# A fused attention and gated convolution kernel: rope in nine GpSimd pieces, and three steps moved between engines

## The chip, the cores and the metric

The kernel runs on one core of a Trainium2 chip. A core has a matrix engine (TensorE, PE in the profile, whose weight loads stand apart as PEld), a vector engine (VectorE, DVE), a scalar engine for activation functions (ScalarE, ACT), a general engine (GpSimd, POOL) and a sync engine that issues transfers (SyncE, SP). Each works through its own queue in order; semaphores tie the queues together. The metric is device microseconds of one execution, as the median of several.

## The reference

Attention over 4 batches of 8 heads, 576 positions and 64 values per head, followed by a gated feed-forward layer:

```python
q_rot, k_rot = (rotate(q), rotate(k))          # rope: cos and sin of position
scores = scale * np.matmul(q_rot, k_rot.transpose(0, 1, 3, 2))
scores = scores - np.max(scores, axis=-1, keepdims=True)
attn = np.exp(scores)
attn = attn / (np.sum(attn, axis=-1, keepdims=True) + 1e-09)
x = np.matmul(attn, v)                          # heads side by side: 512 columns
h = np.maximum(x @ w_in, 0.0)                   # 512 -> 1024
conv_out = sum(conv_w[k] * hp[:, k:k + S, :])   # three taps along the sequence, hp is h padded
gate = 1.0 / (1.0 + np.exp(-conv_out))
return h * gate @ w_out                         # 1024 -> 512
```

Activations are 32-bit floats; the weights arrive as 64-bit floats and are turned on the chip.

## The kernel before

Heads are worked on in pairs, 16 pairs `p`, each in five steps `s` of 128 (the last 64) query rows. A step computes scores on PE (`emit_S`, line 232, into the PSUM tile `sp`), the negated row maximum on DVE (line 240), the exponential with its row sums on ACT (line 244, `st`), and turns the result on PE (`emit_T`, line 289) for ACT to copy out to `pt` (line 170, by `evac`). When a pair's steps are done, `emit_E` multiplies by the values (line 342, two halves, each ending with products that need the remainder rows `pt[:, 8]`, which DVE copies out of PSUM in `emit_Trem`, line 172), `emit_rinv` takes the reciprocal of the row sums on DVE (lines 315, 316), `emit_rinvT` turns it on PE and sends it through DRAM, and the norm on DVE (line 354) applies it.

Ahead of this, a pair's q and k are loaded by SP into `rq` and `rk`, rotated in place on GpSimd by `rope` (line 163 multiplies 1152 columns by the table, line 164 adds two halves into 576 columns), and turned by DVE into `qT` and `kT` (lines 209, 213). `qT` is then scaled in place on ACT (line 170, out and in both `qT`).

The feed-forward layer works in 8 blocks `blk` of 288 rows and 8 slices `f` of 128 hidden columns. `emit_M1` (line 373) makes a slice in three passes, ACT applies the relu into one of four `rr` tiles (line 381), DVE runs the three taps of the convolution (line 385 the first, line 387 the other two), ACT the tanh that makes the gate (line 393), DVE the product with h (line 396), and ACT and GpSimd split it into a high and a low part (lines 404, 405) for `emit_M2` (line 451).

The order is written out by hand: `at(n, rank, fn)` puts a piece of work into step `n` at a rank, and every emission on PE calls `tick`, which first emits what `defer(k, fn)` put off by `k` ticks. So a rank or a lag sets the place in each engine's queue, not a time. Steps below `WIDE` = 26 (about the first 150 us) hold attention and the conversion of the weights on ACT, DVE and GpSimd (lines 469 to 530); from there on attention and feed-forward slices alternate; the last blocks run alone at the end. `late["short"]` is set for the last steps and chooses shorter lags there.

Of the kernel before, what the change touches and what calls it, by code (L numbers as in the profile page):

```python
# [11 lines left out]
AF = mybir.ActivationFunctionType  # L12
ALU = mybir.AluOpType
# [7 lines left out]
def attention_moe_kernel(ctx, tc, q, k, v, w_in, conv_w, w_out, tab, tabx, out):  # L21
    nc = tc.nc
# [7 lines left out]
    HS = S // 2  # L30
# [4 lines left out]
    scale = float(D) ** -0.5  # L35
# [21 lines left out]
    tabt = keep.tile([128, S // 32, 2, 32], F32, name="tabt")  # L57
    idf = keep.tile([128, 128], F32, name="idf")
    cw = keep.tile([128, 32], F32, name="cw")
# [14 lines left out]
    late = {"tail": False, "short": False}  # L74
# [4 lines left out]
    def defer(k, fn, rank=1):  # L79
        due.setdefault(slot[0] + k, []).append((rank, len(due.get(slot[0] + k, [])), fn))  # L80
# [9 lines left out]
    def m_tile():  # L90
        if late["tail"]:
            return psum["t"].tile([128, 512], F32, tag="mt", name="mt")
        return psum["m"].tile([128, 512], F32, tag="m", name="pm")
# [66 lines left out]

    def rope(p, part):
        x = raw[p, part]
        nc.gpsimd.tensor_tensor(out=x, in0=x, in1=tabt, op=ALU.mult)  # L163
        nc.gpsimd.tensor_tensor(out=x[:, :, 0, :], in0=x[:, :, 0, :], in1=x[:, :, 1, :], op=ALU.add)

    QT, KT = {}, {}

    def evac(eng, out, in_, sc=None):
        if eng == "A" or "m" not in psum:
            nc.scalar.activation(out=out, in_=in_, func=AF.Copy, scale=1.0 if sc is None else sc)  # L170
        elif sc is None:
            nc.vector.tensor_copy(out, in_)
        else:
            nc.vector.tensor_scalar(out=out, in0=in_, scalar1=sc, scalar2=None, op0=ALU.mult)

    def qk_tiles(p):
        if p not in QT:
            QT[p] = p2.tile([128, S], F32, tag="qT", name="qT")
            KT[p] = p2.tile([128, S + 64], F32, tag="kT", name="kT")

    def k_rem(p):
        if p * STEPS < WIDE:
            for h in range(2):
                r = slice(64 * h, 64 * h + 64)
                evac("V", krem[p % 2][r, r], KT[p][r, 576:640])
# [19 lines left out]
    def emit_TQ(p, part):  # L205
        qk_tiles(p)
        x = raw.pop((p, part))[:, :, 0, :]
        if part == "q":
            nc.vector.transpose(out=QT[p].rearrange("p (c i) -> p c i", i=32), in_=x)
            defer(1, lambda: evac("A", QT[p], QT[p], scale))  # L210
        else:
            kt = KT[p].rearrange("p (c i) -> p c i", i=32)
            nc.vector.transpose(out=kt[:, 2:20], in_=x)
            nc.vector.transpose(out=kt[:, 0:2], in_=x[:, 16:18])
            k_rem(p)
# [5 lines left out]
    def go(d, key):  # L221
        for fn in d.pop(key):
            fn()
# [89 lines left out]
    def emit_rinv(p):  # L313
        s = p % 2
        nc.vector.tensor_scalar(out=sums[p], in0=sums[p], scalar1=1e-9, scalar2=None, op0=ALU.add)
        nc.vector.reciprocal(out=rvc[s][:, 0:9], in_=sums[p])
# [46 lines left out]
    def emit_M1(blk, f):  # L363
        b, j = divmod(blk, 2)
        g, rr = late["g"], late["rr"]
        ps = m_tile()
        fs = slice(128 * f, 128 * f + 128)
        n = 3 * NK
        i = 0
        for kk in range(NK):  # L370
            xs = xslot[b, kk, j]
            for w, e in ((winh, 0), (winh, 1), (winl, 0)):
                nc.tensor.matmul(  # L373
                    out=ps[:, 0:XW], lhsT=w[:, kk, fs], rhs=xT[:, xs, e, :], start=(i == 0), stop=(i == n - 1)
                )
                i += 1
        if f == NF - 1:
            for kk in range(NK):
                free_slots.append(xslot.pop((b, kk, j)))
        r = rr[(blk * NF + f) % len(rr)]  # L380
        nc.scalar.activation(out=r[:, 1:XW], in_=ps[:, j:j + XW - 1], func=AF.Relu)  # L381
        c = late["pc"].tile([128, HS], F32, tag="c", name="c")

        def conv():
            nc.vector.tensor_scalar(out=c, in0=r[:, j:j + HS], scalar1=cw[:, f:f + 1], scalar2=None, op0=ALU.mult)  # L385
            for e in (1, 2):
                nc.vector.scalar_tensor_tensor(  # L387
                    out=c, in0=r[:, j + e:j + e + HS], scalar=cw[:, 8 * e + f:8 * e + f + 1], in1=c,
                    op0=ALU.mult, op1=ALU.add,
                )  # L390

        def tanh():
            nc.scalar.activation(out=c, in_=c, func=AF.Tanh, scale=0.5)  # L393

        def gate():
            nc.vector.scalar_tensor_tensor(  # L396
                out=c, in0=c, scalar=1.0, in1=r[:, j + 1:j + 1 + HS], op0=ALU.add, op1=ALU.mult
            )

        def split():  # L400
            o = 0
            for dst, n in g_pieces(blk, f):
                hi, lo = dst[:, 0, :], dst[:, 1, :]
                nc.scalar.activation(out=hi, in_=c[:, o:o + n], func=AF.Copy)  # L404
                nc.gpsimd.tensor_tensor(out=lo, in0=c[:, o:o + n], in1=hi.bitcast(F32), op=ALU.subtract)  # L405
                o += n
            ready.add((blk, f))

        lag = (1, 2, 3, 4) if late["short"] else (2, 5, 7, 9)
        for k, fn in zip(lag, (conv, tanh, gate, split)):  # L410
            defer(k, fn)

# [157 lines left out]
    def at(n, rank, fn):  # L570
        plan.setdefault(n, []).append((rank, len(plan.get(n, [])), fn))

    def emit():
        with tc.manual_schedule(engines=engines):
# [17 lines left out]
            for p in range(1, NP):  # L592
                n = STEPS * p
# [6 lines left out]
            for p in range(NP):  # L600
                n = STEPS * p
                for s in range(STEPS):
                    m = n + s
                    first = m < WIDE
                    if m:
                        at(m - 1 if first else m, 0.5 if first else 0, lambda p=p, s=s: emit_S(p, s))
                    at(m, 0.2, lambda p=p, s=s: go(reds, (p, s)))
                    at(m, 0.3 if first else 1.5, lambda p=p, s=s: go(exps, (p, s)))
                    for h in range(2 if s < 4 else 1):
                        at(m + 1, 0 if m + 1 < WIDE else 1, lambda p=p, s=s, h=h: emit_T(p, s, h))  # L610
                for g, e in ((0, 2), (1, 4), (2, 5)):
                    at(n + e, 2, lambda p=p, g=g: emit_Trem(p, g))
                at(n + 4, 4, lambda p=p: emit_E(p, 0))
                at(n + 5, 4, lambda p=p: emit_E(p, 1))
                at(n + 5, 1.7, lambda p=p: emit_rinv(p))
                at(n + 6, 2, lambda p=p: emit_rinvT(p))
                for j in range(2):
                    at(n + 8, 1.7 + j, lambda p=p, j=j: norms.pop((p, j))())
            nw = len(wsteps)
            for i, u in enumerate(wsteps):  # L620
                x = (WIDE - 1) * i // nw
# [120 lines left out]
```

## Time and profile before

| What | Value |
|---|---|
| median of 3 runs | 581.32 us (576.83 to 585.36) |
| profiled execution | 585.31 us, of which the span of instructions is 583.2 us |
| granted TensorE clock, mean | 0.959 |
| PE busy | 513.9 us (88%) |
| DVE busy | 417.5 us (72%) |
| ACT busy | 316.6 us (54%) |
| POOL busy | 241.3 us (41%) |

Busy time is the sum of the spans in which an engine works on an instruction; whatever an instruction waits for after it has started counts as busy. The clock is a share of 2.4 GHz, and is 0.5 in some stretches. Within a stretch the views tell what each engine idled for, and the instruction that ended the idle time.

### The profile page before, as it was taken

How to read it: one execution, taken by the hardware profiler on the slowest of the kernel's cores; microseconds unless marked ns; L12 is line 12 of the kernel's file. 1: busy time of each engine (PE TensorE's matmuls, PEld its weight loads, DVE VectorE, ACT ScalarE, POOL GpSimd, SP SyncE). 2: the span in 40 equal slices, each digit the busy share in tenths (PEclk: the TensorE clock that was granted, in tenths of full speed). 3: DMA queues.
4: the chain of work that ended last, by engine and by line, in shares of the span. 5: the costliest groups of instructions: out<-in, count | busy, mean ns of one | idle time of the engine just before them, and what ended most of it. 6: DMA issues, size and time to landing. Idle time of an engine off the chain costs nothing.

```text
span 583.2 us, 9069 instructions
## 1 busy us (share of the span) xinstructions
PE 513.9 (88%) x3160; PEld 364.0 (62%) x3160; DVE 417.5 (72%) x668; ACT 316.6 (54%) x810; POOL 241.3 (41%) x221
## 2 busy tenths in 40 slices
PE   3597879788895999897998899997998999999997
PEld 1253434344664667674777577674866767779986
DVE  4888778784586958878598848877288847466971
ACT  2678676675654655565546545574255646334530
POOL 3636547554363534427071714545044212142440
PEclk9979989998896999999999989997999999999999
DMA  9774663934422315051513214060240101000001
GB/s 216 138 155 117 150 143 90 197 75 82 81 42 57 67 50 92 8 113 22 113 28 83 59 54 88 17 124 1 77 83 21 41 22 39 22 37 19 1 36 55
DMA packets 138385, 42.51 MB, mean 73 GB/s; under 512 B 131004, under 2 KB 131940, under 8 KB 138340
## 3 DMA queue, kind: packets, MB, share of 16 engines
q1 hardware_dynamic: 136996, 41.54, 32.6%
q8 instruction: 25, 0.41, 0.3%
q10 hardware_dynamic: 1344, 0.39, 0.3%
q14 instruction: 20, 0.16, 0.1%
HBM read 37.12 MB, written 4.79 MB: 72 GB/s over the span
## 4 chain that ended last, share of the span: by engine, by line
PE 58%; DVE 21%; ACT 9%; DMA 5%; issue 4%; SPq 3%; DVEq 0%; ACTq 0%
PE sp L232 12%; PE pm L451 9%; PE tp L342 8%; PE pm L373 8%; PE tp L289 8%; PE mt L451 6%; DVE c L387 5%; PE mt L373 4%; DVE negm L240 4%; DVE c L385 3%; ACT st L244 3%; DVE c L396 2%; ACT pt L170 2%; DMA w<-moe_w_in 1%; DMA rq<-q 1%
## 5 line engine op out<-in xcount | busy, mean ns | idle before, releaser
L170 ACT ACTIVATE pt<-tp 128x512 f32<-128x512 f32 (+2 forms) x164 | 86.3, 557 | 102.7 <-PE tp L289 98.4
L240 DVE TENSOR_REDUCE negm<-sp 128x1 f32<-128x576 f32 x144 | 102.7, 749 | 42.3 <-PE sp L232 41.8
L405 POOL TENSOR_TENSOR g<-c,g 128x288 fp32r<-128x288 f32 (+4 forms) x88 | 56.2, 650 | 169.9 <-ACT g L404 163.6
L232 PE MATMUL sp<-kT,qT 64*128 64x288 f32 (+4 forms) x556 | 111.3, 490 | 15.9 <-ACT st L244 15.9
L244 ACT ACTIVATE st<-sp,negm 128x576 f32<-128x576 f32 x128 | 93.4, 739 | 14.4 <-DVE negm L240 10.7
L387 DVE SCALAR_TENSOR_TENSOR c<-rr,cw,c 128x288 f32<-128x288 f32 x128 | 91.7, 717 | 4.5
L289 PE MATMUL tp<-idf,st 128*128 128x128 f32 x512 | 78.6, 294 | 17.8 <-ACT st L244 11.5
L289 PEld LDWEIGHTS tp<-idf,st 128*128 128x128 f32 x512 | 58.1, 147 | 47.2 <-ACT st L244 17.4
L373 PE MATMUL pm<-xT,winh 128*128 128x290 f32 x384 | 84.5, 312 | 0.5 <-ACT rr L381 0.5
L232 PEld LDWEIGHTS sp<-kT,qT 64*128 64x128 f32 (+1 forms) x556 | 49.5, 184 | 54.4 <-ACT st L244 25.0
L342 PE MATMUL tp<-pt,vm 128*64 128x290 f32 x512 | 71.7, 423 | 3.7 <-ACT pt L170 3.4
L359 POOL TENSOR_TENSOR xT<-xn,xT 128x290 fp32r<-128x290 f32 x32 | 27.5, 880 | 94.2 <-ACT xT L358 92.9
L373 PEld LDWEIGHTS pm<-xT,winh 128*128 128x128 f32 x384 | 62.8, 194 | 1.4 <-ACT rr L381 0.7
L451 PE MATMUL pm<-wouth,g 128*128 128x512 f32 x176 | 62.2, 411 | 0.0
L396 DVE SCALAR_TENSOR_TENSOR c<-c,rr 128x288 f32<-128x288 f32 x64 | 48.6, 759 | 16.8 <-ACT c L393 16.5
L385 DVE TENSOR_SCALAR c<-rr,cw 128x288 f32<-128x288 f32 x64 | 47.4, 741 | 14.8 <-ACT rr L381 14.5
L373 PE MATMUL pm<-xT,winl 128*128 128x290 f32 x192 | 57.5, 300 | 0.0
L342 PEld LDWEIGHTS tp<-pt,vm 128*64 128x64 f32 x512 | 34.7, 140 | 30.0 <-ACT pt L170 5.1
L163 POOL TENSOR_TENSOR rq<-rq,tabt 128x1152 f32<-128x1152 f32 x15 | 40.5, 2700 | 5.5 <-DMA rq<-q 5.5
L393 ACT ACTIVATE c<-c 128x288 f32<-128x288 f32 x64 | 28.4, 444 | 22.6 <-DVE c L387 22.3
L163 POOL TENSOR_TENSOR rk<-rk,tabt 128x1152 f32<-128x1152 f32 x15 | 40.5, 2701 | 0.0
L451 PEld LDWEIGHTS pm<-wouth,g 128*128 128x128 f32 x176 | 33.5, 190 | 9.7 <-issue 2.2
(99 smaller groups left out, 761.9 us busy)
## 6 DMA issues: line engine op xcount, KB each, us to landing
out<-ot SPq DMA_DIRECT2D x17, 256.0 KB, 2.1
rq<-q SPq DMA_DIRECT2D x30, 144.0 KB, 3.2
rq<-q SPq DMA_DIRECT2D x60, 72.0 KB, 2.9
rk<-k SPq DMA_DIRECT2D x30, 144.0 KB, 3.1
rk<-k SPq DMA_DIRECT2D x60, 72.0 KB, 2.9
w<-moe_w_in SPq DMA_DIRECT2D x8, 512.0 KB, 5.0
vm<-v SPq DMA_DIRECT2D x32, 128.0 KB, 2.5
w<-moe_w_out SPq DMA_DIRECT2D x8, 512.0 KB, 4.2
```

Source lines behind the costliest of these rows:

```text
L163: nc.gpsimd.tensor_tensor(out=x, in0=x, in1=tabt, op=ALU.mult)
L170: nc.scalar.activation(out=out, in_=in_, func=AF.Copy, scale=1.0 if sc is None else sc)
L232: nc.tensor.matmul(out=out, lhsT=qt[64 * h:64 * h + 64, c], rhs=kt[64 * h:64 * h + 64, a:a + n], start=True, stop=True)
L240: reds.setdefault((p, s), []).append(lambda: nc.vector.tensor_reduce(out=nm, in_=sc, axis=AX.XY if len(sc.shape) == 3 else AX.X, op=ALU.ma ...
L244: lambda: nc.scalar.activation(out=dst, in_=sc, func=AF.Exp, bias=nm, scale=1.0, accum_out=sm)
L289: nc.tensor.transpose(ps[:, 128 * t:128 * t + 128], st[:, 128 * t:128 * t + 128], idf)
L342: nc.tensor.matmul(out=xp[64 * h:64 * h + 64, 0:XW], lhsT=vmain[p][:, h, i, :] if i < 4 else vrem[:, h, :], rhs=PT[p][:, 2 * i + h if i < ...
L373: nc.tensor.matmul(out=ps[:, 0:XW], lhsT=w[:, kk, fs], rhs=xT[:, xs, e, :], start=(i == 0), stop=(i == n - 1))
L385: nc.vector.tensor_scalar(out=c, in0=r[:, j:j + HS], scalar1=cw[:, f:f + 1], scalar2=None, op0=ALU.mult)
L387: nc.vector.scalar_tensor_tensor(out=c, in0=r[:, j + e:j + e + HS], scalar=cw[:, 8 * e + f:8 * e + f + 1], in1=c, op0=ALU.mult, op1=ALU.add,)
L396: nc.vector.scalar_tensor_tensor(out=c, in0=c, scalar=1.0, in1=r[:, j + 1:j + 1 + HS], op0=ALU.add, op1=ALU.mult)
L451: nc.tensor.matmul(out=ops[tt][:, 0:width], lhsT=g_tile(tt, f, e), rhs=w[:, f, cols], start=(f == 0 and i == 0), stop=(f == NF - 1 and i = ...
```

## The change

Four edits. `rope` is issued as six multiplications of 192 columns and three additions of 6 x 32 columns in place of one of 1152 and one of 576. The scaling of `qT` is put off by five ticks in place of one. The first tap of the convolution is an ACT activation with a scale per partition one tick after the relu, in all but the last steps, and the lags of what follows go from (2, 5, 7, 9) to (2, 4, 5, 6). The reciprocal of the sums moves from rank 1.7 to rank 4.5 of its step.

```diff
--- before.py
+++ after.py
@@ -160,8 +160,12 @@
 
     def rope(p, part):
         x = raw[p, part]
-        nc.gpsimd.tensor_tensor(out=x, in0=x, in1=tabt, op=ALU.mult)
-        nc.gpsimd.tensor_tensor(out=x[:, :, 0, :], in0=x[:, :, 0, :], in1=x[:, :, 1, :], op=ALU.add)
+        for a in range(0, 18, 3):
+            y = x[:, a:a + 3]
+            nc.gpsimd.tensor_tensor(out=y, in0=y, in1=tabt[:, a:a + 3], op=ALU.mult)
+        for a in range(0, 18, 6):
+            y = x[:, a:a + 6]
+            nc.gpsimd.tensor_tensor(out=y[:, :, 0, :], in0=y[:, :, 0, :], in1=y[:, :, 1, :], op=ALU.add)
 
     QT, KT = {}, {}
 
@@ -207,7 +211,7 @@
         x = raw.pop((p, part))[:, :, 0, :]
         if part == "q":
             nc.vector.transpose(out=QT[p].rearrange("p (c i) -> p c i", i=32), in_=x)
-            defer(1, lambda: evac("A", QT[p], QT[p], scale))
+            defer(5, lambda: evac("A", QT[p], QT[p], scale))
         else:
             kt = KT[p].rearrange("p (c i) -> p c i", i=32)
             nc.vector.transpose(out=kt[:, 2:20], in_=x)
@@ -381,8 +385,14 @@
         nc.scalar.activation(out=r[:, 1:XW], in_=ps[:, j:j + XW - 1], func=AF.Relu)
         c = late["pc"].tile([128, HS], F32, tag="c", name="c")
 
+        def tap():
+            nc.scalar.activation(out=c, in_=r[:, j:j + HS], func=AF.Copy, scale=cw[:, f:f + 1])
+
+        short = late["short"]
+
         def conv():
-            nc.vector.tensor_scalar(out=c, in0=r[:, j:j + HS], scalar1=cw[:, f:f + 1], scalar2=None, op0=ALU.mult)
+            if short:
+                nc.vector.tensor_scalar(out=c, in0=r[:, j:j + HS], scalar1=cw[:, f:f + 1], scalar2=None, op0=ALU.mult)
             for e in (1, 2):
                 nc.vector.scalar_tensor_tensor(
                     out=c, in0=r[:, j + e:j + e + HS], scalar=cw[:, 8 * e + f:8 * e + f + 1], in1=c,
@@ -406,7 +416,9 @@
                 o += n
             ready.add((blk, f))
 
-        lag = (1, 2, 3, 4) if late["short"] else (2, 5, 7, 9)
+        if not short:
+            defer(1, tap)
+        lag = (1, 2, 3, 4) if short else (2, 4, 5, 6)
         for k, fn in zip(lag, (conv, tanh, gate, split)):
             defer(k, fn)
 
@@ -612,7 +624,7 @@
                     at(n + e, 2, lambda p=p, g=g: emit_Trem(p, g))
                 at(n + 4, 4, lambda p=p: emit_E(p, 0))
                 at(n + 5, 4, lambda p=p: emit_E(p, 1))
-                at(n + 5, 1.7, lambda p=p: emit_rinv(p))
+                at(n + 5, 4.5, lambda p=p: emit_rinv(p))
                 at(n + 6, 2, lambda p=p: emit_rinvT(p))
                 for j in range(2):
                     at(n + 8, 1.7 + j, lambda p=p, j=j: norms.pop((p, j))())
```

The order of DVE's queue at the end of a pair, before the change (the 64x64 copy is of the remainder rows that the second half of `emit_E` needs; `rr_1323` and `rr_1324` are two of the four relu tiles, `c` the convolution):

```order
L396 SCALAR_TENSOR_TENSOR c<-c,rr_1323 128x288
L385 TENSOR_SCALAR c<-rr_1324,cw 128x288
L387 SCALAR_TENSOR_TENSOR c<-rr_1324,cw,c 128x288 x2
L240 TENSOR_REDUCE negm<-sp 128x1 x2
L315 TENSOR_SCALAR sums<-sums 128x9
L316 RECIPROCAL rvc_82<-sums 128x9
L172 COPY pt<-tp 64x64 x2
L396 SCALAR_TENSOR_TENSOR c<-c,rr_1324 128x288
```

and the same place in the changed kernel (line numbers are 4 to 12 higher; `rr_1407` and `rr_1408` are the same two relu tiles):

```order
L406 SCALAR_TENSOR_TENSOR c<-c,rr_1407 128x288
L176 COPY pt<-tp 128x256
L397 SCALAR_TENSOR_TENSOR c<-rr_1408,cw,c 128x288 x2
L244 TENSOR_REDUCE negm<-sp 128x1 x2
L176 COPY pt<-tp 64x64 x2
L406 SCALAR_TENSOR_TENSOR c<-c,rr_1408 128x288
L319 TENSOR_SCALAR sums<-sums 128x9
L320 RECIPROCAL rvc_82<-sums 128x9
```

The first tap has left the queue, and the copies now come straight behind the two maxima, with sums and reciprocal behind them.

The order of ACT's queue where a pair's `qT` is scaled, before:

```order
L170 ACTIVATE pt<-tp 128x4x128 x2
L404 ACTIVATE g<-c 128x224
L404 ACTIVATE g<-c 128x64
L170 ACTIVATE qT<-qT 128x576
L244 ACTIVATE st,sums<-sp,negm 128x576 x2
L170 ACTIVATE pt<-tp 128x4x128 x2
L244 ACTIVATE st,sums<-sp,negm 128x576 x2
L381 ACTIVATE rr_1321<-pm 128x289
L170 ACTIVATE pt<-tp 128x4x128 x2
L393 ACTIVATE c<-c 128x288
```

and now:

```order
L174 ACTIVATE pt<-tp 128x4x128 x2
L248 ACTIVATE st,sums<-sp,negm 128x576 x2
L174 ACTIVATE qT<-qT 128x576
L174 ACTIVATE pt<-tp 128x4x128 x2
L248 ACTIVATE st,sums<-sp,negm 128x576 x2
L385 ACTIVATE rr_1405<-pm 128x289
L389 ACTIVATE c<-rr_1405,cw 128x288
L174 ACTIVATE pt<-tp 128x4x128
L403 ACTIVATE c<-c 128x288
L174 ACTIVATE pt<-tp 128x4x128
```

The scaling stands behind the two exponentials, and the tap (line 389) stands behind its relu. The tanh (line 403) stands ahead of a copy to `pt` that it stood behind.

## Rows read from the trace of the kernel before

**Rows 1.** Two stretches: length, busy us (count) per engine, PEclk, DMA share, GB/s.

```profile
20.00:150.00 130.00, 102.36 (x576) 53.35 (x574) 101.05 (x148) 93.40 (x230) 74.75 (x47) 0.92 0.56 122
150.00:500.00 350.00, 324.61 (x2089) 237.38 (x2088) 253.82 (x402) 190.03 (x488) 134.79 (x129) 0.96 0.27 58
```

**Rows 2.** What PE waited for, 150 to 500 us: total, times, longest.

```profile
PE sp L232 <- ACT st L244: 13.9, 11, 6.4
PE tp L342 <- DVE pt L172: 8.6, 4, 2.5
PE tp L342 <- ACT pt L170: 2.8, 6, 0.5
```

**Rows 3.** Timeline, a pair ends: start us, us, engine, line, tiles, xcount, [idle <-releaser].

```profile
264.27 1.51 DVE L396 SCALAR_TENSOR_TENSOR c<-c,rr 128x288 f32<-128x288 f32 x1 [1.20 <-ACT c L393]
...
264.95 1.24 PE L232 MATMUL sp<-kT,qT 64*128 64x288 f32 x8
...
265.70 1.50 DVE L385 TENSOR_SCALAR c<-rr,cw 128x288 f32<-128x288 f32 x1
...
267.25 1.50 DVE L387 SCALAR_TENSOR_TENSOR c<-rr,cw,c 128x288 f32<-128x288 f32 x2
...
268.67 1.41 DVE L240 TENSOR_REDUCE negm<-sp 128x1 f32<-128x576 f32 x2
268.88 2.61 POOL L163 TENSOR_TENSOR rk<-rk,tabt 128x1152 f32<-128x1152 f32 x1
...
270.00 1.53 DVE L315 TENSOR_SCALAR sums<-sums 128x9 f32<-128x9 f32 x1
...
271.69 0.40 DVE L172 COPY pt<-tp 64x64 f32<-64x64 f32 x2
...
272.14 0.71 PE L342 MATMUL tp<-pt,vr 128*64 128x290 f32 x4 [2.51 <-DVE pt L172]
```

**Rows 4.** Timeline, the step after a pair ends.

```profile
301.19 0.80 POOL L405 TENSOR_TENSOR g<-c,g 128x288 fp32r<-128x288 f32 x1 [2.62 <-ACT g L404]
...
301.95 2.64 POOL L163 TENSOR_TENSOR rk<-rk,tabt 128x1152 f32<-128x1152 f32 x1
...
302.50 2.40 DVE L396 SCALAR_TENSOR_TENSOR c<-c,rr 128x288 f32<-128x288 f32 x1
...
304.83 1.51 DVE L385 TENSOR_SCALAR c<-rr,cw 128x288 f32<-128x288 f32 x1
...
307.90 1.42 DVE L240 TENSOR_REDUCE negm<-sp 128x1 f32<-128x576 f32 x2
...
310.04 0.68 ACT L170 ACTIVATE qT<-qT 128x576 f32<-128x576 f32 x1 [1.69 <-DVE qT L209]
...
310.63 0.72 ACT L244 ACTIVATE st<-sp,negm 128x576 f32<-128x576 f32 x1
...
311.50 1.96 PE L232 MATMUL sp<-kT,qT 64*128 64x288 f32 x8 [1.60 <-ACT st L244]
```

**Rows 5.** Timeline, two DVE operations while POOL is idle.

```profile
316.69 0.45 DVE L396 SCALAR_TENSOR_TENSOR c<-c,rr 128x288 f32<-128x288 f32 x1
...
317.75 1.07 DVE L387 SCALAR_TENSOR_TENSOR c<-rr,cw,c 128x288 f32<-128x288 f32 x2
```

**Rows 6.** Timeline, the start of a rope, and DVE beside it.

```profile
173.18 0.82 DVE L396 SCALAR_TENSOR_TENSOR c<-c,rr 128x288 f32<-128x288 f32 x1 [1.34 <-ACT c L393]
173.65 2.87 POOL L163 TENSOR_TENSOR rk<-rk,tabt 128x1152 f32<-128x1152 f32 x1
...
173.93 2.76 DVE L385 TENSOR_SCALAR c<-rr,cw 128x288 f32<-128x288 f32 x1
```

**Rows 7.** Groups by line and shape, ACT: count, busy us, mean ns, idle before.

```profile
L393 ACT ACTIVATE c<-c 128x288 f32<-128x288 f32 x64 | 28.4, 444 | 22.6 <-DVE c L387 22.3
```

**Rows 8.** Timeline, DVE turns a q in the first 150 us.

```profile
46.20 0.78 DVE L209 STREAM_TRANSPOSE qT<-rq 128x576 f32<-128x576 f32 x1 [1.30 <-POOL rq L164]
```

**Rows 9.** Stretch with a lowered clock (columns of rows 1).

```profile
400.00:409.00 9.00, 7.86 (x30) 5.37 (x31) 4.59 (x9) 3.48 (x9) 2.84 (x4) 0.62 0.00 0
```

## The prediction

> **What bounds the kernel now.** The page's busy shares come first: PE is busy for 88% of the span, DVE for 72%, ACT for 54%, POOL for 41%. So PE carries the time, and what can be gained is PE's idle time and the time that it works at a lowered clock. The view by stretches says where the idle time lies [rows 1]: from 20 to 150 us PE is busy for 102.4 of 130 us (27.6 idle), from 150 to 500 for 324.6 of 350 (25.4 idle). The diff leaves the feed-forward slices of the end as they were (the old branch for short lags), so the time after 500 us is left alone here.
>
> The view of waits breaks the 25.4 us down almost without remainder [rows 2]: scores wait for an exponential (13.9 us, 11 times, one of them 6.4), the second product with the values waits for DVE's copy of the remainder rows (8.6 us, 4 times), the first product for ACT's copies (2.8 us, 6 times). None of these names GpSimd. The timeline does. Where a pair ends, DVE takes 1.51 us for the gate product, 1.50 for the first tap and 1.50 for two more taps [rows 3]; with POOL idle the gate product takes 0.45, the two taps 1.07 together [rows 5]. In another pair the gate product starts at 302.50, inside a rope multiplication that runs from 301.95 to 304.59, takes 2.40 and ends 0.31 after it; the tap behind it is held up again, for 1.51 in all [rows 4]. So a DVE operation that meets a rope instruction stands still until it has nearly ended (0.45 of work against 0.31 of overhang: it starts some 0.14 us before the recorded end). Operations that read PSUM aren't held: maxima behind it run at 0.7 each [rows 3, 4].
>
> What follows from it is seen in the same rows. In rows 3 the scores are there at 264.95 + 1.24 = 266.2, but DVE gets to their maxima only at 268.67; behind these stands the sums' operation, 1.53 us beside the next rope; then the copy, and PE goes on at 272.14 after 2.51 us of idle time. In rows 4 the maxima end at 309.3, but ACT's exponential starts at 310.63, since the scaling of q stands ahead of it and had waited 1.69 us for DVE to turn q; PE goes on at 311.50 after 1.60 us.
>
> **The change, part by part.**
>
> Rope pieces. A GpSimd instruction of 288 columns takes 0.80 us, one of 1152 takes 2.64 [rows 4]: 1.84 / 864 = 2.13 ns a column, so 192 columns are 0.80 - 0.20 = 0.60 us. Nine are 5.4; the two old ones are 2.64 and, by the same line, 1.41, so a rope grows by 1.35 us, 30 ropes by 40 us. POOL is busy for 135 of 350 us [rows 1], and in that stretch nothing of rows 2 waits for it. A DVE operation that meets a piece now waits at most 0.60 - 0.14 = 0.46 us, at the least nothing; I take the upper end, since the operations of rows 3 and 4 stand close behind each other and the next piece starts when one is through. A gate product then costs 0.9, two taps 2.0.
>
> The copy's gap (rows 3, done again). From 264.27: gate product 0.9, the other copy that now stands here 0.4, two taps 2.0, so the maxima start at 267.6 and not at 268.67, and end at 269.0; the copy comes directly behind them, as the sums have moved, and ends at 269.4. PE was through with what came before at 272.14 - 2.51 = 269.6. The gap is gone. Of the 8.6 us I leave 0.6: **-8.0**, between -4 and -8.6.
>
> The exponential's gap (rows 4). From 302.50: gate product 0.9, two taps 2.0 without the first, sums and reciprocal 0.8, so maxima at 306.2 and through at 307.6; the scaling no longer stands ahead of the exponential, which starts at 307.7 and not at 310.63; PE's scores follow it by 0.9 as they do now, at 308.6, before PE is free for them (311.50 - 1.60 = 309.9). The gap is gone. The one long wait stands behind a rope beside which the first tap took 2.76 us [rows 6]: without that tap, and with 0.46 in place of a whole instruction for the taps behind it, some 4.5 of 6.4 us come back. Of the other 7.5 us I leave 1.0. **-11.0**, between -5.5 and -13.
>
> The tap on ACT. Five blocks of eight slices take it, 40 in all. An activation of this shape with constant operands takes 0.444 us [rows 7]; the tap has a scale per partition. At 576 columns the exponential, which has a bias per partition, takes 0.72 and the scaling of q, which has none, 0.68 [rows 4], so I add 0.04: 0.48 us, 19 us on ACT, whose 350 us hold 190 of work [rows 1]. That is hidden in its sum, but copies to `pt` stand behind tap and tanh now, and PE's 2.8 us of waits for them may double: **+2.8**, between 0 and +7 (0.48 us at a third of 40, or so).
>
> The Trainium skill speaks against this edit a little more strongly than the row: "ScalarE: Activation LUTs", What ACT_TABLE_LOAD costs, has each per-partition operand add about 93 ns. The rows say 40 ns, though one of them reads PSUM and the other doesn't; by that figure of the Trainium skill the tap would be an estimated 0.54 us, and the sum at most 2 us higher, were every tap on PE's path.
>
> Before 150 us. There is no tap yet, and the queue to turn q is tight: DVE already waited 1.30 us for a rope once [rows 8]. Five ropes of q, 1.35 us longer each, cost at most 6.8. On the other side a blocked conversion gets shorter, as the gate product of rows 4 does (2.40 to 0.9, 1.5 us), at most once for each of four pairs on the path: 6. I set the two against each other: 0, between -6 and +6.8.
>
> The clock. Behind PE's gaps stand stretches at 1.2 GHz: from 400 to 409 us the granted clock is 0.62, so 9 x 0.38 / 0.5 = 6.8 us at the lower level, with PE busy for 7.9 of the 9 [rows 9]. From 150 to 500 us the mean is 0.96 [rows 1], 28 us at the lower level; half of that, less the idle time inside, is lost, some 8 us. Fewer gaps may mean fewer of these: between 0 and -8, I take **-4**.
>
> The sum: 585.3 (the profiled execution) - 8.0 - 11.0 + 2.8 + 0 - 4 = 565.1. That execution lies 4.0 above the median of 581.3 and at the top of three that spread by 8.5; I take these 4.0 to be clock as well, so that against the median the clock's term is already in: 581.3 - 16.2 = 565.1 again. The predicted time is **565 us**, the range of this case 553 to 574.
>
> **The rivals.**
>
> *The gaps come back elsewhere.* DVE's wait gets shorter, but PE waits next for ACT, and the longer rope holds up q in the first 150 us. Half of the 19 us return and the 6.8 are lost: 581.3 - 9.5 + 6.8 = 578.6. For it: rows 8, and ACT's longer queue. Against it: both reconstructed gaps close with 0.2 to 1.3 us to spare. Chance 0.25.
>
> *DVE doesn't get in between the pieces*, so that the change doesn't do what it says. Then an operation waits for the whole 5.4 us in place of 2.64, while the one behind it is free (some 1.1 saved): 1.7 us more at each of 20 ropes, 34; with three quarters of it on the path, as the 15 gaps of 8.6 and 13.9 us suggest, +25, less 9 for the edits that don't hang on rope: 597. Against it: the multiplication starts at 173.65 [rows 6] straight behind another GpSimd instruction, and the gate product beside it, 0.82 from 173.18, still ended at 174.0, while the multiplication took 2.87 and not 2.64; the DVE operation had come in between. "GPSIMD Engine Reference", Instruction dispatch, in the Trainium skill lets each of the engine's cores start the next instruction as soon as its own share is done, with which there need be no moment between two pieces. By that rule it is this case; the trace disagrees in rows 6. Chance 0.05.
>
> *The gate waits for ACT*, which is the slower end. Its place in DVE's queue is now three ticks behind the taps and one behind the tanh, where it was five and two; maxima and copies stand behind it, and ACT has the tap to do. Such a wait is already there once in rows 3, 1.20 us. At 30 of 40 slices on the path this is 36 us: 565 + 36 = 601. It decides against the change when the tanh ends on average over 0.5 us after DVE is ready for the gate (40 x 0.5 = 20 us, all that was gained). Against it: maxima (1.4 us) stand between taps and gate at most places, and the tanh is 0.44. Chance 0.08.
>
> **The numbers.** 0.62 for the forecast, 0.25, 0.05 and 0.08 for the rivals. Two per cent of the median is 11.6 us, about what a measurement of this kernel can tell from no change. Below 569.7 lies most of the forecast's case (0.55) and a little of the first rival (0.02): 0.57 faster. Above 592.9 lie the second and third rival, nearly whole: 0.12 slower. The rest, 0.31, is within 2%. The range of 552 to 582 takes in the forecast's case and the larger part of the first rival.
>
> **What the profile after would show.** Right: rope pieces of about 0.60 us; taps with a mean of 0.6 to 0.7 and gate products of about 0.6, none over 1.1; PE waits from 150 to 500 us of about 8 us in place of 25; exponentials that start directly behind their maxima. The tap on ACT near 0.48. Wrong: DVE operations of 2 us and more beside a run of pieces (second rival); DVE idle before the gate, released by ACT's tanh, in tens of us (third); DVE idle before it turns q, released by POOL, of over 5 us (first). My forecast is most easily wrong by the waits on ACT, of which no row of before shows the new order.

## The result: 32 us faster, twice what was forecast

The changed kernel takes 548.71 us (median of 4 runs, 546.33 to 549.59) against 580.86 for the kernel before, run beside it: a ratio of 0.944 (95% interval 0.936 to 0.952), 32 us. The prediction was 565, with a range from 552: the direction and the mechanism came as forecast, but the forecast gain was only half of the measured one, and the time lies just below the range.

The profiled execution took 547.9 us, with a span of 546.1 (583.2 before). The first lines of its profile page:

```profile
span 546.1 us, 9259 instructions
PE 503.4 (92%) x3160; PEld 357.5 (65%) x3160; DVE 350.7 (64%) x628; ACT 331.0 (61%) x850; POOL 279.5 (51%) x431
```

PE's 3160 matmuls are the same ones. They took 513.9 us before and take 503.4 now: 10.5 us less for the same work, which is the clock (mean granted clock 0.959 before, 0.977 now). PE's idle time fell from 583.2 - 513.9 = 69.3 to 546.1 - 503.4 = 42.7, by 26.6. So 37.1 us of span are 26.6 of idle time and 10.5 of clock. (The medians differ by less, 32 us: the profiled execution of before is 4.4 us longer than its median.)

The two stretches that answer to [rows 1]: length, busy us (count) for PE, PEld, DVE, ACT, POOL, then granted clock, DMA share, GB/s.

```profile
20.00:150.00 130.00, 107.42 (x606) 56.83 (x604) 93.59 (x151) 94.80 (x233) 94.24 (x135) 0.91 0.58 125
150.00:500.00 350.00, 343.22 (x2274) 256.85 (x2272) 218.16 (x407) 215.36 (x561) 164.05 (x262) 1.00 0.27 60
```

From 150 to 500 us PE now idles for 6.8 us, not 25.4, at a mean clock of 1.00, not 0.96; DVE is busy for 36 us less. From 20 to 150 us it idles for 22.6, not 27.6, although POOL has 20 us more to do there.

What PE waited for from 150 to 500 us, which answers to [rows 2] (total, times, longest):

```profile
PE tp L346 <- ACT pt L174: 2.8, 6, 0.5
PE sp L236 <- ACT st L248: 2.0, 9, 0.5
```

The waits for DVE's copy (8.6 us) are gone altogether, those for the exponential fell from 13.9 to 2.0, those for ACT's copies stayed at 2.8. The 1.9 us that remain of 6.8 are three waits of the feed-forward layer, of the same lengths as three that before came after 500 us.

The timeline where the pair of [rows 3] ends (start us, us, engine, line, operation, tiles, shapes, count, idle time before it and its releaser; in order of start):

```profile
247.33 1.07 DVE L397 SCALAR_TENSOR_TENSOR c<-rr,cw,c 128x288 f32<-128x288 f32 x2 [1.34 <-ACT c L389]
...
247.99 3.82 POOL L165 TENSOR_TENSOR rq<-rq,tabt 128x192 f32<-128x192 f32 x6
...
248.75 1.42 DVE L244 TENSOR_REDUCE negm<-sp 128x1 f32<-128x576 f32 x2 [0.34 <-PE sp L236]
...
249.99 2.17 PE L346 MATMUL tp<-pt,vm 128*64 128x290 f32 x16 [0.47 <-ACT pt L174]
...
250.09 0.45 DVE L176 COPY pt<-tp 64x64 f32<-64x64 f32 x2
...
250.56 0.80 DVE L406 SCALAR_TENSOR_TENSOR c<-c,rr 128x288 f32<-128x288 f32 x1
...
251.28 0.56 DVE L319 TENSOR_SCALAR sums<-sums 128x9 f32<-128x9 f32 x1
...
251.99 0.66 PE L346 MATMUL tp<-pt,vr 128*64 128x290 f32 x4
```

DVE waits for scores at 248.4 now (0.34 us), where before the scores waited for DVE. The copy is done at 250.54, and PE comes to its rows at 251.99, straight out of other work: 1.4 us to spare. The gate product in the middle of six rope pieces takes 0.80, the sums 0.56, not 1.53.

The place of [rows 4]:

```profile
280.73 0.63 DVE L406 SCALAR_TENSOR_TENSOR c<-c,rr 128x288 f32<-128x288 f32 x1
...
283.12 1.64 DVE L397 SCALAR_TENSOR_TENSOR c<-rr,cw,c 128x288 f32<-128x288 f32 x2 [0.84 <-ACT c L389]
...
285.57 1.42 DVE L244 TENSOR_REDUCE negm<-sp 128x1 f32<-128x576 f32 x2
...
287.47 0.74 ACT L248 ACTIVATE st<-sp,negm 128x576 f32<-128x576 f32 x1
...
289.63 0.76 PE L236 MATMUL sp<-kT,qT 64*128 64x288 f32 x4
289.95 0.70 ACT L174 ACTIVATE qT<-qT 128x576 f32<-128x576 f32 x1
```

The exponential stands ahead of the scaling of q, and PE's next scores come 1.4 us after its end with no wait. The same operations by line and shape (count, busy us, mean ns, idle time before), first the taps and the gate product in the kernel before, then the changed kernel:

```profile
L387 DVE SCALAR_TENSOR_TENSOR c<-rr,cw,c 128x288 f32<-128x288 f32 x128 | 91.7, 717 | 4.5
L396 DVE SCALAR_TENSOR_TENSOR c<-c,rr 128x288 f32<-128x288 f32 x64 | 48.6, 759 | 16.8 <-ACT c L393 16.5
```

```profile
L397 DVE SCALAR_TENSOR_TENSOR c<-rr,cw,c 128x288 f32<-128x288 f32 x128 | 85.0, 664 | 39.6 <-ACT c L389 36.5
L406 DVE SCALAR_TENSOR_TENSOR c<-c,rr 128x288 f32<-128x288 f32 x64 | 35.2, 550 | 9.4 <-ACT c L403 9.1
L319 DVE TENSOR_SCALAR sums<-sums 128x9 f32<-128x9 f32 x16 | 7.3, 458 | 0.0
L389 ACT ACTIVATE c<-rr,cw 128x288 f32<-128x288 f32 x40 | 21.6, 539 | 0.2
L165 POOL TENSOR_TENSOR rq<-rq,tabt 128x192 f32<-128x192 f32 x90 | 56.0, 655 | 6.1 <-DMA rq<-q 6.1
```

A tap costs 0.66 us on the mean (0.72 before) and a gate product 0.55 (0.76 before); beside an idle POOL they take 0.53 and 0.45 [rows 5]. A new wait stands in the first line: DVE idles for 36.5 us in all for ACT's tap. No wait of PE follows from it, and the kernel that keeps the tap on DVE is as fast (the first experiment below).

### The profile page after: what moved, and what is told of

Read it like the earlier page. It is cut to its first block, busy times and chain, and to the rows that moved or that the text cites. A ratio compares the mean times of both kernels' runs of the same rounds, so it can differ in the third digit from the quotient of the medians.

```text
span 546.1 us, 9259 instructions
## 1 busy us (share of the span) xinstructions
PE 503.4 (92%) x3160; PEld 357.5 (65%) x3160; DVE 350.7 (64%) x628; ACT 331.0 (61%) x850; POOL 279.5 (51%) x431
## 4 chain that ended last, share of the span: by engine, by line
PE 69%; ACT 9%; DVE 6%; DMA 4%; issue 4%; SPq 3%; POOL 3%; POOLq 0%; DVEq 0%; ACTq 0%
PE sp L236 14%; PE tp L346 13%; PE pm L463 11%; PE pm L377 10%; PE tp L293 9%; PE mt L463 6%; PE mt L377 5%; ACT pt L174 4%; ACT st L248 3%; POOL rq L165 2%; DVE negm L244 1%; DVE c L397 1%; SPq L125 1%; DMA rq<-q 1%; PE tp L305 1%
## 5 line engine op out<-in xcount | busy, mean ns | idle before, releaser
L236 PE MATMUL sp<-kT,qT 64*128 64x288 f32 (+4 forms) x556 | 108.5, 484 | 3.0 <-ACT st L248 3.0
L397 DVE SCALAR_TENSOR_TENSOR c<-rr,cw,c 128x288 f32<-128x288 f32 x128 | 85.0, 664 | 39.6 <-ACT c L389 36.5
L293 PE MATMUL tp<-idf,st 128*128 128x128 f32 x512 | 75.2, 285 | 14.6 <-ACT st L248 8.4
L293 PEld LDWEIGHTS tp<-idf,st 128*128 128x128 f32 x512 | 55.8, 143 | 42.4 <-issue 14.4
L236 PEld LDWEIGHTS sp<-kT,qT 64*128 64x128 f32 (+1 forms) x556 | 47.2, 180 | 38.7 <-issue 15.9
L165 POOL TENSOR_TENSOR rq<-rq,tabt 128x192 f32<-128x192 f32 x90 | 56.0, 655 | 6.1 <-DMA rq<-q 6.1
L165 POOL TENSOR_TENSOR rk<-rk,tabt 128x192 f32<-128x192 f32 x90 | 54.3, 637 | 0.0
L406 DVE SCALAR_TENSOR_TENSOR c<-c,rr 128x288 f32<-128x288 f32 x64 | 35.2, 550 | 9.4 <-ACT c L403 9.1
L354 ACT ACTIVATE xn<-tp 128x290 f32<-128x290 f32 x32 | 13.2, 413 | 42.8 <-PE tp L346 34.8
L377 PEld LDWEIGHTS pm<-xT,winl 128*128 128x128 f32 x192 | 36.7, 191 | 0.0
```

What stands on the lines that cost most here:

```text
L165: nc.gpsimd.tensor_tensor(out=y, in0=y, in1=tabt[:, a:a + 3], op=ALU.mult)
L236: nc.tensor.matmul(out=out, lhsT=qt[64 * h:64 * h + 64, c], rhs=kt[64 * h:64 * h + 64, a:a + n], start=True, stop=True)
L293: nc.tensor.transpose(ps[:, 128 * t:128 * t + 128], st[:, 128 * t:128 * t + 128], idf)
L377: nc.tensor.matmul(out=ps[:, 0:XW], lhsT=w[:, kk, fs], rhs=xT[:, xs, e, :], start=(i == 0), stop=(i == n - 1))
L397: nc.vector.scalar_tensor_tensor(out=c, in0=r[:, j + e:j + e + HS], scalar=cw[:, 8 * e + f:8 * e + f + 1], in1=c, op0=ALU.mult, op1=ALU.add,)
L406: nc.vector.scalar_tensor_tensor(out=c, in0=c, scalar=1.0, in1=r[:, j + 1:j + 1 + HS], op0=ALU.add, op1=ALU.mult)
```

## Experiments

Theory A throughout: the rope pieces let waiting DVE operations in, this closes most of PE's gaps, and a higher clock follows from closed gaps. Theory B: the gain comes from the tap and the two moved operations, with the pieces as a help at most.

**One part alone.** Kernel before, and only the rope in nine pieces:

```diff
-        nc.gpsimd.tensor_tensor(out=x, in0=x, in1=tabt, op=ALU.mult)
-        nc.gpsimd.tensor_tensor(out=x[:, :, 0, :], in0=x[:, :, 0, :], in1=x[:, :, 1, :], op=ALU.add)
+        for a in range(0, 18, 3):
+            ...  # six products of 192 columns
+        for a in range(0, 18, 6):
+            ...  # three sums of 192 columns
```

> Before with the nine rope pieces as its only edit. Theory A (a DVE operation that meets rope waits for one whole GpSimd instruction, so smaller instructions free the queue; the PE gaps close by that, and the stretches at 1.2 GHz go with the gaps): redoing rows 3 with all four operations still on DVE gives a gap of about 1.0 us in place of 2.5 and no gap in rows 4, so PE waits of about 10 us in place of 25 from 150 to 500 us, and a time of 560 to 567. Rival B (the gaps close because work left DVE's queue or moved behind what PE waits for; the size of the pieces matters little, since nine short waits add up to two long ones): 574 to 581, PE waits still over 18 us. In both: DVE operations beside rope never above 1.1 us.

Measured: 548.67 us, 0.943 (0.937 to 0.950), the whole gain of the full change; both expectations were too high. Its waits on PE from 150 to 500 us, and DVE's lines there:

```profile
PE tp L346 <- ACT pt L174: 2.9, 6, 0.5
PE sp L236 <- ACT st L248: 2.6, 7, 1.3
```

```profile
L391 DVE SCALAR_TENSOR_TENSOR c<-rr,cw,c 128x288 f32<-128x288 f32 x104 | 68.2, 655 | 3.7
...
L400 DVE SCALAR_TENSOR_TENSOR c<-c,rr 128x288 f32<-128x288 f32 x51 | 31.4, 616 | 17.9 <-ACT c L397 17.7
...
L389 DVE TENSOR_SCALAR c<-rr,cw 128x288 f32<-128x288 f32 x52 | 26.7, 513 | 12.4 <-ACT rr L385 11.8 <-POOL rk L165 0.4
```

With the tap still on DVE, the sums ahead of the copy and the scaling of q ahead of the exponential, the waits are nearly the same as in the changed kernel. The pieces alone are enough, so theory B, by which they help at most, falls here.

The tap on ACT and the shorter lags alone:

```diff
+        def tap():
+            nc.scalar.activation(out=c, in_=r[:, j:j + HS], func=AF.Copy, scale=cw[:, f:f + 1])
...
+        if not short:
+            defer(1, tap)
-        lag = (1, 2, 3, 4) if late["short"] else (2, 5, 7, 9)
+        lag = (1, 2, 3, 4) if short else (2, 4, 5, 6)
```

> Before with the first tap on ACT and the new lags as its only edit. Theory A: the tap saves 0.4 to 1.5 us of DVE ahead of the maxima in a pair, but the 2.4 us blocks stay: 568 to 575. Rival B: 555 to 562, PE waits from 150 to 500 us under 10 us.

Measured: 560.56, 0.964 (0.957 to 0.971), within B's range and below A's. PE waits:

```profile
PE sp L232 <- ACT st L244: 6.2, 11, 3.0
PE tp L342 <- ACT pt L170: 2.8, 6, 0.5
PE tp L342 <- DVE pt L172: 2.6, 4, 0.8
```

The two moves alone:

```diff
-            defer(1, lambda: evac("A", QT[p], QT[p], scale))
+            defer(5, lambda: evac("A", QT[p], QT[p], scale))
-                at(n + 5, 1.7, lambda p=p: emit_rinv(p))
+                at(n + 5, 4.5, lambda p=p: emit_rinv(p))
```

> Before with the scaling of q and the sums later, rope and tap untouched. Theory A: takes the sums' 1.5 to 2 us out of the copy's gap (8.6 us down to about 3) and the scaling out of the exponential's (each some 1 us in 10): 568 to 574. Rival B: 560 to 567.

Measured: 564.01, 0.971 (0.964 to 0.978), again within B's range and below A's; the exponential's waits are down to 2.7 us, the copy's to 2.3, and one new wait of 3.6 us appears. So each part alone shortens the same gaps: 34, 22 and 18 us against the kernel before in the same comparison, 74 in sum, while all together give 32, which is within the intervals what the pieces give alone. The parts don't add up, since a gap that one of them has closed can't be closed again. Theory A was right that the pieces close the gaps, and underrated what the other edits do without them.

**One part taken back.** The changed kernel with the two whole rope instructions of before:

> The changed kernel with the two whole rope instructions back. Theory A: 2.4 us blocks are back, the maxima and copies behind them late: 558 to 566, stretches at 1.2 GHz back after 150 us. Rival B: 549 to 553, PE waits after 150 us under 8 us.

Measured: 556.99, 0.958 (0.952 to 0.965), between the two forecasts: the other two parts together give 25 us, the pieces the last 8. No stretch at 1.2 GHz came back after 150 us, against what A said (granted clock 1.00 there), and no gap of PE there is longer than 1.3 us. The changed kernel with the tap on DVE (`if True:` in place of `if short:`, no `defer(1, tap)`), with the scaling of q at `defer(1, ...)`, and with the sums at rank 1.7:

> The changed kernel with the first tap back on DVE at the head of the convolution, lags as changed. Theory A: each tap costs DVE 0.37 to 0.83 us ahead of the maxima; the reconstructed gaps had 0.2 to 1.3 us to spare, so some come back: 550 to 556. Rival B (the tap's leaving carries the gain): 560 and more.

> The changed kernel with the scaling of q one tick after its transpose again, ahead of the exponentials. Theory A: the exponential is late by the transpose's wait and 0.68 us, some 1 to 2 us at ten pairs, of which PE had about 1 to spare: 550 to 558. Rival B: 555 to 562.

> The changed kernel with the sums' reciprocal ahead of the copies of the remainder rows again. With short pieces the sums' operation takes at most 0.6 us and the reciprocal 0.2, against some 0.2 us to spare: gaps of 0.5 us at four to ten pairs, 549 to 553 by theory A. Rival B: 555 and more.

Measured: 547.77 (0.943, 0.939 to 0.947), 549.48 (0.946, 0.942 to 0.950), 548.13 (0.943, 0.939 to 0.948), all below what both theories forecast. Once the rope is in pieces, none of the three edits is worth anything that can be measured.

**How long a piece should be.** Two whole instructions for pairs 1 to 6 and pieces from pair 7 on (`3 if p > 6 else 18`, `6 if p > 6 else 18` as the steps of the two loops):

> The changed kernel with whole rope instructions for pairs 1 to 6, whose rope runs in the first 150 us, and pieces from pair 7 on. Tells whether the pieces help or hurt in the first 150 us: there DVE now waits 7.0 us for rope before it turns q (1.3 before), while its conversions are blocked for less. If the lateness decides, 544 to 547; if the shorter blocks do, 550 to 553; if they cancel, as I forecast, 547 to 550.

Measured: 551.99, 0.951 (0.946 to 0.956), some 3 to 4 us behind (the kernels at 547.77 and 548.13 above were run beside it). So the pieces help before 150 us too, where a term of 0 had been set. The conversions of the weights there, in the kernel before, in the changed kernel and in this one (20 to 150 us):

```profile
L486 DVE SCALAR_TENSOR_TENSOR wf<-w,wt 128x512 int32<-128x512 int32 x16 | 17.2, 1077 | 0.6
```

```profile
L498 DVE SCALAR_TENSOR_TENSOR wf<-w,wt 128x512 int32<-128x512 int32 x16 | 13.1, 816 | 0.6
...
L484 DVE TENSOR_SCALAR wt<-wt 128x512 f32<-128x512 f32 x16 | 9.8, 613 | 0.0
```

```profile
L499 DVE SCALAR_TENSOR_TENSOR wf<-w,wt 128x512 int32<-128x512 int32 x16 | 15.3, 954 | 0.6
L485 DVE TENSOR_SCALAR wt<-wt 128x512 f32<-128x512 f32 x16 | 11.6, 725 | 0.0
```

Coarser: five pieces, three products of 384 columns and two sums of 288 (steps 6 and 9).

> The changed kernel with five pieces, three of 384 and two of 288 columns, in place of nine of 192. If a DVE operation waits for one instruction, the longest blocked one is about 1.0 us longer than its free time, and PE's gaps stay closed by what the other edits leave to spare: 547 to 551. If the number of pieces counts as such: 553 and more.

Measured: 548.86, 0.947 (0.940 to 0.953), as with nine and as forecast. Finer: 27 pieces of 64 columns (steps 1 and 2).

> The changed kernel with 27 pieces of 64 columns. By the GpSimd rows of before a piece takes about 0.32 us, a rope 8.6 us and more in place of 5.4: the longest block falls to 0.2 us, but q's rope comes 3 us later in the first 150 us, where DVE already waits 7 us for it: 550 to 558. If short blocks are all that counts: 545 to 548.

Measured: 571.06, 0.983 (0.975 to 0.992), 22 us slower than nine pieces and above both forecasts. All of it is lost early: the 900th matmul ends at 213.6 us here and at 189.3 with nine pieces. A place in its timeline:

```profile
26.71 5.02 POOL L166 TENSOR_TENSOR rk<-rk,tabt 128x64 f32<-128x64 f32 x18
...
28.80 3.86 DVE L499 SCALAR_TENSOR_TENSOR wf<-w,wt 128x512 int32<-128x512 int32 x1
...
31.69 3.07 POOL L169 TENSOR_TENSOR rk<-rk 128x64 f32<-128x64 f32 x9
```

One DVE operation takes 3.86 us, 28.80 to 32.66, and POOL goes through the last of its eighteen products and into its nine sums meanwhile. Three more stand for over 2 us, the longest for 4.02. But a rope is also longer, 8.3 us as a median against 5.5 with nine pieces, and DVE waits for it (20 to 190 us; 7.0 with nine pieces):

```profile
DVE qT L214 <- POOL rq L169: 17.0, 4, 6.3
```

How the 22 us divide between held operations and the longer rope was not taken apart.

In the middle: 15 pieces, nine products of 128 columns and six sums of 96 (steps 2 and 3).

> The changed kernel with fifteen pieces, nine multiplications of 128 columns and six additions of 96. With 64 columns DVE operations stood still through a whole run of pieces (3.9 us once), with 192 never. If the run of pieces lets DVE in between from 128 columns on: 548 to 552, no DVE operation beside rope above 1.2 us. If not: operations of 2 to 4 us in the first 190 us and 555 to 570.

Measured: 556.87, 0.959 (0.955 to 0.964), 8 us behind nine pieces, again all before 150 us, and within the second forecast. A long stand happens there too, once, and DVE's wait for q's rope is longer here as well (10.1 us):

```profile
48.80 3.79 POOL L165 TENSOR_TENSOR rk<-rk,tabt 128x128 f32<-128x128 f32 x9
...
50.90 5.26 DVE L484 TENSOR_SCALAR wt<-wt 128x512 f32<-128x512 f32 x1
52.51 2.15 POOL L168 TENSOR_TENSOR rk<-rk 128x96 f32<-128x96 f32 x6
...
54.58 1.30 POOL L542 TENSOR_TENSOR winl<-wf,winh 128x512 fp32r<-128x512 f32 x1
```

A conversion that takes 0.61 on the mean in the changed kernel stands from 50.90 to 56.16, while nine whole pieces and an uncut GpSimd operation of 512 columns behind them pass. In the kernels whose pieces all have 192 columns or more, a whole piece passed inside a held DVE operation four times, one piece each and 0.92 us at most; beside the nine pieces of the changed kernel the longest conversion took 1.18 us. So the prediction's second rival (DVE doesn't get in) is real, but for shorter pieces, and not at each of them.

**The turn of q.** DVE now waits longer for the rope before it turns q (7.0 us, 3 times, longest 3.8; 1.3 before). The changed kernel with that turn one step later in pairs 2 to 6:

```diff
-                    at(max(n - 4 + 2 * i, 2), 0.45, lambda p=p, part=part: emit_TQ(p, part))
+                    at(max(n - 4 + 2 * i + (i == 0 and 1 < p < 7), 2), 0.45, lambda p=p, part=part: emit_TQ(p, part))
```

> The changed kernel with q's turn on DVE one step later in pairs 2 to 6, whose rope is late. If DVE's 7.0 us of waiting for rope in the first 150 us hold PE up there: 542 to 546. If PE is held up by other things there (weights, exponentials): 546 to 550.

Measured: 553.92, 0.956 (0.948 to 0.964), 5 us worse and above both forecasts. PE's wait from 20 to 150 us for the scaled q, which is 1.6 us, once, in the changed kernel:

```profile
PE sp L259 <- ACT qT L174: 12.7, 5, 3.8
```

DVE's idle time there is covered; a later turn makes q late for PE.

**What a gap costs.** The changed kernel with one more DVE operation ahead of the copies of the remainder rows from pair 7 on: a maximum over weight columns, whose result nothing uses. First 2048 columns, 2.2 us:

```diff
+            if p > 6:
+                nc.vector.tensor_reduce(out=late["idle"], in_=winh[:, 0:2, :].bitcast(F32), axis=AX.XY, op=ALU.max)
```

> The changed kernel with 2.2 us more of DVE work (a maximum over 2048 columns of weights, which doesn't use its result) ahead of the copies of the remainder rows, in pairs 7 to 15: an idle stretch of PE of some 2 us is put back at nine places and nothing else is touched. Tells whether a gap costs its own length or brings the lower clock with it. Theory A: PE's idle time after 150 us grows by 14 to 20 us and the time by more than that, 566 to 576, with stretches at 1.2 GHz back. Rival (the lower clock came from something else in the kernel before, not from the gaps): the time grows by the idle time alone, 562 to 568, and the clock stays at 1.00.

Measured: 553.87, 0.955 (0.948 to 0.962). Both forecasts missed, because the gaps were small, so this run alone doesn't say what a gap does to the clock. It does show that the added operation by itself doesn't lower it (0.981 in its profile, 1.00 from 150 to 500 us):

```profile
PE tp L349 <- DVE pt L177: 2.8, 5, 0.7
```

An operation of 2.2 us made gaps of at most 0.7: the copy had some 1.5 us to spare, as in the timeline above. So 4096 columns, 4.4 us (`0:4`):

> As the run with 2.2 us more of DVE work ahead of the copies, with 4.4 us (4096 columns). The shorter one left gaps of only 0.6 us at five places, so PE has some 1.6 us to spare there; now gaps of 2 to 3 us at five to nine places, as in the kernel before: idle time after 150 us up by 12 to 20 us. Theory A (gaps bring the lower clock): 10 to 30 us at 1.2 GHz come back after 150 us, and the time grows by 5 to 12 us more than the idle time does, 566 to 578. Rival (the lower clock has another cause): clock 1.00 after 150 us, the time grows by the idle time, 560 to 568.

Measured: 581.41, against 579.96 for the kernel before, 1.001 (0.997 to 1.005): the whole gain is gone, with the pieces, the tap and the moves all in place. The waits, and one place:

```profile
PE tp L349 <- DVE pt L177: 20.1, 8, 2.8
```

```profile
423.81 4.41 DVE L313 TENSOR_REDUCE idle<-winh 128x1 f32<-128x4096 f32 x1
424.22 2.18 PE L349 MATMUL tp<-pt,vm 128*64 128x290 f32 x16
...
428.14 0.45 DVE L177 COPY pt<-tp 64x64 f32<-64x64 f32 x2
...
428.64 1.22 PE L349 MATMUL tp<-pt,vr 128*64 128x290 f32 x4 [2.24 <-DVE pt L177]
```

Eight gaps of 2.2 to 2.8 us sum to 20.1. The four matmuls behind this one take 1.22 us, and 0.66 in the changed kernel. The reason is the clock. In this profile three stretches at 1.2 GHz stand after 150 us, ahead of the last few us, each directly behind one of the eight gaps (columns of rows 1); in the changed kernel's there is none:

```profile
227.30:230.70 3.40, 3.25 (x12) 1.48 (x12) 2.31 (x5) 0.41 (x1) 3.40 (x7) 0.50 0.01 2
322.90:326.30 3.40, 3.25 (x12) 1.48 (x12) 0.85 (x4) 0.74 (x2) 1.06 (x2) 0.50 0.02 5
428.70:432.10 3.40, 3.40 (x13) 1.49 (x14) 1.98 (x4) 0.41 (x1) 3.40 (x6) 0.50 0.00 0
```

The profiled execution, 574.64 us, was the fastest of ten. Its span is 26.8 us longer than the changed kernel's: PE idles 20.9 us longer and is busy 5.9 us longer for the same matmuls. The medians differ by more, 32.7 us, at a lower clock: most of the ten runs had a mean of 0.958 to 0.961 (the highest 0.972), the changed kernel's 0.977 to 0.981. A mean of 0.960 over 579 us is 579 x 0.040 / 0.5 = 46 us at 1.2 GHz, one of 0.979 some 23; half of the difference, 12 us, is an estimate of what the median run loses by the clock, and 20.1 + 12 = 32. That gaps bring the lower clock is shown by this run, together with the one before it; A's 566 to 578 was still 3 us too low, and the rival's 560 to 568 is ruled out.

## Why the prediction was wrong

Right was the reading of the wait: DVE operations stand still beside a long GpSimd instruction, shorter pieces let them in, and both reconstructed gaps close. A piece of 0.60 us was forecast and takes 0.59 where nothing disturbs it. The sizes were wrong. By terms, in us, for the profiled execution:

| term | forecast | measured |
|---|---|---|
| gap before the copy | -8.0 | -8.6 |
| gap before the exponential | -11.0 | -11.9 |
| tap on ACT, PE's wait for ACT's copies | +2.8 | 0.0 |
| before 150 us | 0 | -6.1 |
| clock (PE busy for the same matmuls) | -4 | -10.5 |
| sum | -20.2 | -37.1 |

Of the 16.9 us that the forecast missed, 1.5 are in the gaps, 2.8 in ACT's copies, 6.1 before 150 us and 6.5 in the clock. The steps that failed:

- **"I take these 4.0 to be clock as well, so that against the median the clock's term is already in."** This set the clock's gain at zero against the median. With the next term it is the largest of the errors. The medians differ by 32.2; with 26.6 of idle time, some 6 remain for the clock. The runs of before in the last comparison have clocks of 0.956 to 0.976, so that lowered stretches are a trait of the kernel before and not of its one profiled execution. In that execution's trace five stretches at 1.2 GHz stand after 150 us, 27 us in sum, each beginning in a gap of 1.6 to 6.4 us or within 2.2 us of its end; all five are gone, where -4 took half of what they cost. The long-gap experiment shows the link: on top of its own length, each microsecond of such gaps cost 0.3 us by the clock in the profiled execution and an estimated 0.6 in the median run.
- **"I set the two against each other: 0."** Before 150 us the rope's extra 1.35 us did make DVE wait (7.0 in place of 1.3), but this was covered; the shorter holding of the conversions (line 498 of the changed kernel: 816 ns on the mean, 1077 before, 954 in the mixed kernel) counted for more, and 6.1 us came: 1.1 in the first 20 us, 5.0 up to 150 [rows 1]. The mixed kernel gives some 3 to 4 of them to the pieces. The rest may be chance: the kernel with the tap alone does the same work as the kernel before until the feed-forward slices begin, and its profiled execution ends the 639th matmul at 152.2 us, before's at 156.1, the changed kernel's at 151.2.
- **"+2.8" for the tap on ACT.** The waits for ACT's copies are 2.8 us before and after [rows 2]. The tap takes 0.539 us, not 0.48. "ScalarE: Activation LUTs", What ACT_TABLE_LOAD costs, in the Trainium skill has 93 ns for each per-partition operand, and 0.444 + 0.095 is what the rows show [rows 7]: the page was nearer than the forecast's 40 ns. None of it reached PE, though DVE now waits 36.5 us for this tap.
- **"At most 0.46 us, I take the upper end."** The held time per operation was far less on the mean: taps 664 ns against 517 for the fastest in the same trace, gate products 550 against 414. The forecast's two taps at 2.0 us and gate at 0.9 are at the level of a bad case (1.64 and 0.80 above). As a bound it didn't hold either: the slowest tap took 1.17 us, and a piece beside DVE's work itself took up to 1.14.
- **The range.** It ended at 552 for want of adding the favourable ends of its own terms: 581.3 - 8.6 - 13 + 0 - 6 - 8 = 545.7 (549.7 from the profiled execution) would have been in it.

The prediction's sentence "Operations that read PSUM aren't held" is right but too narrow. The turns of q read and write SBUF and take 0.77 us in the kernel before, with GpSimd at work beside them all the time or not at all; the maximum over 4096 columns in SBUF takes 4.41 us in all nine cases, with GpSimd idle or busy throughout. Held were the taps, the gate products, the sums' operation and the conversions.

The rivals: the gaps did not return elsewhere; the two waits named in rows 2 shrank and no new one stands in their place. That DVE isn't let in between pieces is false at 192 columns (0.944) and true in part at 64 to 128 (3.86 and 5.26 us). "GPSIMD Engine Reference", Instruction dispatch, in the Trainium skill lets the engine's cores start the next instruction without a common stop; the long stands beside shorter pieces agree with that, the rows of 192 columns and more don't show it. That the gate waits for ACT came to 9.1 us of DVE's idle time in all (16.5 before), and PE's waits for the exponentials behind DVE's maxima, where it would show, are 2.0 us. The sign named for the first rival, over 5 us of DVE's waiting for rope before it turns q, did appear (7.0), without the loss that it was to stand for: PE waited 1.6 us for the scaled q.

What the profile didn't let one see beforehand is that the pieces alone would do: the forecast credited the tap and the moves with a share of each gap, while the first experiment has the same waits without them, and taking them back one at a time costs nothing. That the moves matter without the pieces (18 us) and not with them fits the slack: with pieces the copy ends 1.4 us before PE comes to its rows, more than the 0.56 that the sums would take ahead of it.

What stays open: what decides whether a piece of 64 to 128 columns lets DVE in, since many do; how much of the loss with 15 and 27 pieces is the longer rope; and why some gaps of PE bring the lower clock and others of the same length do not (three of eight in the long-gap profile did).

## What to carry to other kernels

Where elementwise DVE operations on SBUF tiles (here scalings, sums and products, not maxima or turns) take several times their free time, look at the timeline for a long GpSimd instruction beside them, and cut that into pieces of a few hundred columns before reordering anything: here five or nine pieces gave the whole gain, 27 lost most of it. Price a PE gap at more than its length where the granted clock falls behind it, and take that price from stretches of the same kernel, not from the distance of one execution to the median. When several edits aim at the same gaps, their gains don't add: run each alone and each taken back.

## What the runs showed of the hardware

Beside a run of short GpSimd instructions (64 to 128 columns of 128 partitions) a DVE operation can stand through nine whole pieces and the operation behind them, 5.26 us, longer than beside the uncut instruction (3.00 us at most in the kernel before); with pieces of 192 columns and more a held operation let one piece pass at most. Maxima and turns on DVE weren't held (4.41 and 0.77 us, with GpSimd busy beside them or idle). Eight gaps of 2.2 to 2.8 us on PE, 20.1 us in sum, cost 26.8 us in the profiled execution and 32.7 by the medians.
